# First input chunks in three transfers on two queues, zero-padded kv and wo, two products left over in the last block, in a gated attention and MLP kernel

## The chip, the core and the metric

The kernel runs on one core of a Trainium2 chip. What counts is the device time of one execution in microseconds (us). Before the change it is 435.35 us, the median of three runs (435.15 to 435.68).

The engines are named as in the profile: PE multiplies matrices and writes PSUM, PEld is its loading of weights, DVE, ACT and POOL work element by element, SP issues most transfers from memory. A row with a q behind the engine (SPq, ACTq) is an instruction of that engine's sequencer, here a transfer being issued.

## The reference

2048 rows of 448 floats go through a linear attention (16 heads of 28) and through an MLP with 1792 hidden columns and a squared ReLU; a sigmoid gate mixes both.

```python
g = sigmoid((x * gate_w).sum(-1, keepdims=True))
q, k, v = split(x @ wqkv)                       # 16 heads of 28
phi = lambda t: where(t > 0, t + 1, exp(t)) + 1e-6
kv  = einsum("bhsd,bhse->bhde", phi(k), v)
z   = phi(k).sum over s
o   = (phi(q) @ kv) / (phi(q) . z + 1e-6)
a   = o.reshape(B, S, D) @ wo
h   = relu(x @ w1 + b1)
b   = (h * h) @ w2 + b2
return g * a + (1 - g) * b
```

## The kernel before, in words

Everything is float32, and each operand of a product is split into two float32r halves, a high part (a conversion, `split_hi`, L63) and a low part (the subtraction of it, `split_lo`, L71). A product is then three terms: high by high, high by low, low by high. The 448 input columns are four chunks of 128 rows (`c` = 0 to 3); the fourth holds its 64 columns twice, with both parts stacked, and needs two terms. So one tile of hidden columns is 11 matmuls of 512 columns (`up`, L241, through `up_chunk`, L218), and the same 11 terms occur in queries, keys and attention.

The rows go in four blocks of 512 (`b`, `TB` = 512, `NB` = 4). In a first pass each block makes the first seven of 14 tiles of hidden columns: `up`, then `hidden` (L231: ReLU and square on ACT, split on DVE), then `down` (L260: 12 matmuls of 448 columns into four PSUM banks `o_ps`). Between them stand the keys (`keys`, L291) and the sums of phi(k) times x (`gram`, L331). After the pass `kv_product` (L397) makes kv; `split_kv` splits it, and `m_product` (L431) multiplies it by a quarter of wo four times, three matmuls each, into the matrix `m_s` that `attention` (L512) uses. In the second pass, in the order 3, 0, 1, 2, each block makes the other seven tiles, its queries (`queries`, L447), denominators and attention, and `finish` (L275) writes the rows out. `n` counts the blocks of the second pass and `fl` the tiles in one.

The order on PE, ACT and DVE is that of the code. SP and POOL are placed by the scheduler of the tile framework, which also hands out eight semaphores for transfers in turn: the ninth issue waits until the first has landed. `down` queues its 12 matmuls in a list (`owed`), and `leave` says how many of them stay in the list until the next `down`; they then run behind the next `up`. The tables `leaves` (L616 for the first pass, L683 for the second) give that number by block and tile.

The start, on which much of the change bears: PE first runs 14 matmuls on constants (L177). Two transfers `xw` (L184 to L187), 256 KB each, bring half the columns of x's chunk 0 beside half the columns of the first weights' chunk 0. ACT converts the x half, DVE the weight half, and four matmuls of 256 columns (L547) follow, for two tiles by two column halves. The other products of chunk 0 are ordered by terms (for `n`, L555), those of chunks 1 to 3 tile by tile (L559). `split_x` (L111) and `split_w1` (L141) convert chunks 1 to 3, high parts on ACT and low parts on DVE.

kv has 112 rows a head group (`JE`), so the tiles `kv_h`, `kv_l`, `woh` and `wol` have 112 partitions.

Of the kernel before, what the change touches and what calls it, by code (L numbers as in the profile page):

```python
# [7 lines left out]
F = mybir.dt.float32  # L8
# [7 lines left out]
P = 128  # L16
TB = 512
# [10 lines left out]


@with_exitstack  # L30
def gated_mix_kernel(ctx: ExitStack, tc: tile.TileContext, xw, xt, xn, wk, wq, wv, wo, w1a, w1b, w2, b1, b2, gw,
                     hmask, kvmask, halves, out):
    nc = tc.nc
    act, dve, pool, pe, sp = nc.scalar, nc.vector, nc.gpsimd, nc.tensor, nc.sync
# [93 lines left out]

    w1_s, w1_raw = {}, {}

    def load_w1(h, g, c):
        w1_raw[h, g, c] = slot([P, (TB, 3 * P)[g]], F, f"w1r{h}{g}{c}")
        load(w1_raw[h, g, c], (w1a, w1b)[g][h, c])

    def new_w1(h, g):
        n, a, z = ((TB, 0, 16), (3 * P, 48, 0))[g]
# [39 lines left out]
    for _ in range(14):  # L176
        pe.matmul(warm_ps[:, :256], warm[:, :P], warm, start=True, stop=True)  # L177

    side = rest.tile([P, 56], F, name="side")[:, :2]
    dve.memset(side[:64, 0:1], -1.0)  # L180
    dve.memset(side[:64, 1:2], 0.0)
    dve.memset(side[64:], 1.0)

    xw_raw = []  # L184
    for n in range(2):
        xw_raw.append(slot([P, TB], F, f"xwr{n}"))
        load(xw_raw[n], xw[n])  # L187
    for c in range(1, 4):
        load_x(0, c)
        load_w1(0, 0, c)  # L190
    b1_s = keep.tile([P, NF], F, name="b1_s")
    half = keep.tile([P, 2], F, name="half")
    ones = keep.tile([P, 2], F, name="ones")
# [193 lines left out]
    def load_kv(c):  # L387
        if c == 0:
            kvm.append(slot([JE, D], F, "kvm"))
            load(kvm[0], kvmask)  # L390
        wv_s.append(slot([P, D], F, f"wv{c}"))
        load(wv_s[-1], wv[c])

    def kv_product():
        kv_ps = bank("kv_ps")
        z_ps = mm_p.tile([P, 512], F, name="z_ps", tag="mm")
        for c in range(4):  # L397
            pe.matmul(z_ps[:, 2 * c:2 * c + 2], zks[0][:, c].rearrange("p j r -> p (j r)"), ones, start=True,  # L398
                      stop=True)
        dve.tensor_copy(zc, z_ps[:, 0:8:2])  # L400
        for j in range(NJ):
            js = slice(j * JE, (j + 1) * JE)
            for c in range(4):
                pe.matmul(kv_ps[:JE, js], wv_s[c][:, js], gsum[c][:, js], start=(c == 0), stop=(c == 3))  # L404
        raw = slot([JE, D], F, "kv_raw")
        dve.tensor_tensor(raw, kv_ps[:JE, :D], kvm[0], op=ALU.mult)
        return raw.rearrange("p (j k) -> p j k", j=NJ)

    def split_kv(raw):
        kv.extend([late_tile([JE, NJ, P], "kv_h"), late_tile([JE, NJ, P], "kv_l")])  # L410
        split_hi(act, kv[0][:, :, :JE], raw)
        split_lo(dve, kv[1][:, :, :JE], raw, kv[0][:, :, :JE])
        for t in kv:
            dve.tensor_copy(t[:, :, JE:], f32(t[:, :, 96:JE]))

    def late_tile(shape, name, dt=R):
        return late.tile(shape, dt, name=name, tag="q", bufs=NLATE)
# [1 line left out]
    wo_raw, wo_s = {}, {}  # L419

    def load_wo(j):
        wo_raw[j] = slot([JE, D], F, f"wor{j}")
        load(wo_raw[j], wo[j])

    def split_wo(j):
        wo_s[j] = [late_tile([JE, TB], f"wo{p}{j}")[:, 16:16 + D] for p in "hl"]
        raw = wo_raw.pop(j)
        split_hi(act, wo_s[j][0], raw)
        split_lo(dve, wo_s[j][1], raw, wo_s[j][0])
# [104 lines left out]

    first = [mm_p.tile([P, 512], F, name=f"h_ps0_{f}", tag="mm") if f < 2 else bank(f"h_ps0_{f}") for f in range(4)]
    for c in range(4):
        if c == 0:
            xs[0] = new_x(0)  # L540
            w, (xh, xl) = new_w1(0, 0), [x[:, 0] for x in xs[0]]
            sides = slice(0, TB // 2), slice(TB // 2, TB)
            for n, cols in enumerate(sides):
                split_hi(act, xh[:, cols], xw_raw[n][:, sides[0]])
                split_hi(dve, w[:, 0, cols], xw_raw[n][:, sides[1]])
                for f in range(2):
                    pe.matmul(first[f][:, cols], w[:, 0, f * P:(f + 1) * P], xh[:, cols], start=(n == 0), stop=False)  # L547
            for m, (lo, hi) in enumerate(((xl, xh), (w[:, 4], w[:, 0]))):
                for n, cols in enumerate(sides):
                    split_lo(dve, lo[:, cols], xw_raw[n][:, sides[m]], hi[:, cols])  # L550
        else:
            split_x(0, c)
            split_w1(0, 0, c)
        if c == 0:
            for n in range(3):  # L555
                for f in range(0 if n else 2, 4):
                    up_chunk(first[f], 0, f, c, n)
        else:
            for f in range(4):  # L559
                up_chunk(first[f], 0, f, c)  # L560
    split_w2(0)
    split_w2(1)
    wk_s = keep.tile([P, 7, D], R, name="wk_s", tag="wkm", bufs=1)
# [116 lines left out]


    order = [NB - 1, *range(NB - 1)]
    leaves = (0, 1, 2, 0, 1, 2, 0), (0, 1, 2, 0, 0, 0, 2)  # L683
    late = m_s = None
    for n, b in enumerate(order):
        then = order[n + 1] if n + 1 < NB else None
        for f in range(NF - NH, NF):
            fl = f - NH
            run_todo()
            if fl == (0 if n else 4) and n != 1:  # L690
                split_den(b)
            up(b, f)
            if then is not None and n and fl < 2:
                load_x(then, 2 * fl)
                load_x(then, 2 * fl + 1)
            if n == 0:
                if 1 <= fl < 3:
                    load_x(then, 2 * fl - 2)
                    load_x(then, 2 * fl - 1)
                if fl == 1:  # L700
                    for c in range(4):
                        split_w1(1, 1, c)
                    for j in range(2, 4):
                        load_wo(j)
                if 1 <= fl < 5:
                    split_wo(fl - 1)
                if fl < 2:
                    load_w2(NH + 5 + fl)
                if fl < 3:
                    split_w2(NH + 4 + fl)  # L710
                if 2 <= fl < 4:
                    split_x(then, 2 * fl - 4)
                    split_x(then, 2 * fl - 3)
            elif then is not None and 1 <= fl < 3:
                split_x(then, 2 * fl - 2)
                split_x(then, 2 * fl - 1)
            if fl:
                if n + 1 < NB or f + 1 < NF:
                    down(b, f - 1, leave=leaves[min(n, 1)][fl])
            elif n == 0:  # L720
                down(b, NH - 1)
                half_done(b)
            else:
                down(order[n - 1], NF - 1)
                for i in range(4):
                    if n == 1:
                        attention(order[0], i)
                        if i == 1:
                            split_den(b)
                    finish(order[n - 1], i)  # L730
            if n == 0:
                if fl < 4:
                    todo += queries(b, (3, 0, 1, 2)[fl])
                if fl == 0:
                    for c in range(4):
                        load_w1(1, 1, c)
                    raw = kv_product()
                    phase1.close()
                    late = ctx.enter_context(tc.tile_pool(name="late", bufs=1, side="right", reuse_waits="tile"))
                    m_s = keep.tile([P, 7, D], R, name="m_s", tag="wkm", bufs=1)  # L740
                    split_kv(raw)
                    for j in range(2):
                        load_wo(j)
                if fl == 4:
                    m_product(2)
                if fl in (2, 3, 5):
                    m_product(fl - 2)
                for c in ((0,), (1, 2, 3))[fl - 5] if fl >= 5 else ():
                    scaled(b, c)
                if fl >= 4:  # L750
                    for c in ((3,), (0,), (1, 2))[fl - 4]:
                        todo += queries(then, c)
                if fl == 4:
                    todo += denominators(b)
            else:
                if fl == 0:
                    todo += denominators(b)
                if 2 <= fl < 4:
                    scaled(b, 2 * fl - 4)
# [69 lines left out]
```

## Time and profile before

| | us |
|---|---|
| median of three runs | 435.35 (435.15 to 435.68) |
| the profiled execution | 435.59 |
| its span, first to last instruction | 433.8 |
| PE busy in the span | 429.5 (99%) |
| DVE, ACT, POOL busy | 283.7, 174.5, 72.1 |

The profiled execution is 0.24 us above the median, and 1.8 us of it lie outside the span. Busy time of PE is the union of matmuls that overlap: a matmul of 512 columns is shown with some 390 ns, but the next one starts 227 ns after it. So a stretch of PE is best read by the starts of its matmuls, or by the chain of work that ended last, which gives the time that each run of matmuls added.

### The profile page before, as it was taken

How to read it: one execution, taken by the hardware profiler on the slowest of the kernel's cores; microseconds unless marked ns; L12 is line 12 of the kernel's file. 1: busy time of each engine (PE TensorE's matmuls, PEld its weight loads, DVE VectorE, ACT ScalarE, POOL GpSimd, SP SyncE). 2: the span in 40 equal slices, each digit the busy share in tenths (PEclk: the TensorE clock that was granted, in tenths of full speed). 3: DMA queues.
4: the chain of work that ended last, by engine and by line, in shares of the span. 5: the costliest groups of instructions: out<-in, count | busy, mean ns of one | idle time of the engine just before them, and what ended most of it. 6: DMA issues, size and time to landing. Idle time of an engine off the chain costs nothing.

```text
span 433.8 us, 5561 instructions
## 1 busy us (share of the span) xinstructions
PE 429.5 (99%) x2052; PEld 381.4 (88%) x2052; DVE 283.7 (65%) x462; ACT 174.5 (40%) x302; POOL 72.1 (17%) x93
## 2 busy tenths in 40 slices
PE   9999999999999999999999999999999999999996
PEld 7898999898989899898898888988888888888986
DVE  5899518843499437784449777887653967457624
ACT  6865324421346122453145443444433434233421
POOL 0045006500065002540010441000100001000000
PEclk9999999999999999999999999999999999999999
DMA  7741302020221211223244321130101301002002
GB/s 282 240 134 51 109 0 69 27 68 1 70 82 65 72 45 48 65 58 111 63 118 134 69 65 38 61 122 0 26 0 48 136 0 26 0 0 86 0 2 85
DMA packets 18347, 29.00 MB, mean 67 GB/s; under 512 B 2896, under 2 KB 12672, under 8 KB 18320
## 3 DMA queue, kind: packets, MB, share of 16 engines
q1 hardware_dynamic: 16416, 26.35, 19.5%
q0 software_dynamic: 1760, 2.20, 2.3%
q8 instruction: 16, 0.26, 0.3%
q14 instruction: 11, 0.09, 0.1%
q10 hardware_dynamic: 144, 0.10, 0.1%
HBM read 22.31 MB, written 3.67 MB: 60 GB/s over the span
## 4 chain that ended last, share of the span: by engine, by line
PE 98%; DMA 1%; DVE 0%; ACT 0%; DVEq 0%; issue 0%
PE h_ps L229 32%; PE o_ps L254 31%; PE q_ps L84 8%; PE k_ps L254 8%; PE a_ps L84 8%; PE g_ps L84 8%; PE kv_ps L404 1%; DMA xwr<-in_xw 1%; PE m_ps L84 1%; PE d_ps L84 0%; PE h_ps L547 0%; PE z_ps L398 0%; DVE out L278 0%; ACT xh L65 0%; DVEq L825 0%
## 5 line engine op out<-in xcount | busy, mean ns | idle before, releaser
L254 PE MATMUL o_ps<-w,hh 128*128 128x448 f32 x448 | 128.6, 362 | 0.0
L229 PE MATMUL h_ps<-xh,w 128*128 128x512 f32 x390 | 124.8, 391 | 0.0
L254 PEld LDWEIGHTS o_ps<-w,hh 128*128 128x128 f32 x448 | 84.0, 187 | 7.7
L229 PE MATMUL h_ps<-xl,w 128*128 128x512 f32 x224 | 87.0, 391 | 0.0
L229 PEld LDWEIGHTS h_ps<-xh,w 128*128 128x128 f32 x390 | 73.4, 188 | 14.1
L254 PE MATMUL o_ps<-w,hl 128*128 128x448 f32 x224 | 81.2, 362 | 0.0
L233 ACT ACTIVATE hr<-h_ps,b_s 128x512 f32<-128x512 f32 x56 | 38.1, 680 | 86.1 <-PE h_ps L229 80.8
L69 DVE CAST hh<-hr 128x512 fp32r<-128x512 f32 x56 | 23.5, 420 | 61.8 <-ACT hr L234 61.7
L229 PEld LDWEIGHTS h_ps<-xl,w 128*128 128x128 f32 x224 | 42.4, 189 | 8.0
L254 PEld LDWEIGHTS o_ps<-w,hl 128*128 128x128 f32 x224 | 42.0, 188 | 3.7
L72 DVE TENSOR_TENSOR hl<-hr,hh 128x512 fp32r<-128x512 f32 x56 | 39.7, 709 | 3.3
L72 POOL TENSOR_TENSOR nl<-xnr,nh 128x384 fp32r<-128x384 f32 x16 | 17.2, 1076 | 119.0 <-ACT nh L65 118.9
L234 ACT ACTIVATE hr<-hr 128x512 f32<-128x512 f32 x56 | 35.4, 632 | 1.8
L84 PE MATMUL q_ps<-xh,wq_s 128*128 128x512 f32 x100 | 33.1, 390 | 0.0
L84 PE MATMUL a_ps<-m_s,qh 128*128 128x448 f32 x112 | 32.7, 362 | 0.0
L254 PE MATMUL k_ps<-wk_s,xh 128*128 128x448 f32 x112 | 32.7, 361 | 0.0
L474 POOL DMA_DIRECT2D qr<-qv x16 | 7.9, 503 | 124.3 <-ACT qv L471 94.5
L72 DVE TENSOR_TENSOR pl<-r,ph 128x448 fp32r<-128x448 f32 x16 | 23.7, 1479 | 0.0
L327 POOL TENSOR_TENSOR ksum<-ksum,r 128x448 f32<-128x448 f32 x15 | 23.3, 1555 | 1.1 <-DVE r L289 1.1
L84 PE MATMUL q_ps<-xl,wq_s 128*128 128x512 f32 x60 | 23.4, 389 | 0.0
L254 PE MATMUL k_ps<-wk_s,xl 128*128 128x448 f32 x64 | 23.2, 363 | 0.0
L84 PE MATMUL a_ps<-m_s,ql 128*128 128x448 f32 x64 | 23.2, 362 | 0.0
(111 smaller groups left out, 565.8 us busy)
## 6 DMA issues: line engine op xcount, KB each, us to landing
xr<-in_xt SPq DMA_DIRECT2D x27, 256.0 KB, 2.7
xnr<-in_xn SPq DMA_DIRECT2D x16, 224.0 KB, 2.5
out<-out SPq DMA_DIRECT2D x15, 224.0 KB, 1.9
w2r<-in_w SPq DMA_DIRECT2D x14, 224.0 KB, 2.7
w1r<-in_w1a SPq DMA_DIRECT2D x7, 256.0 KB, 2.7
w1r<-in_w1b SPq DMA_DIRECT2D x8, 192.0 KB, 3.3
m_s<-m POOLq DMA_DIRECT2D x12, 112.0 KB, 2.5
wqr<-in_wq SPq DMA_DIRECT2D x4, 256.0 KB, 2.7
```

Source lines behind the costliest of these rows:

```text
L69: eng.tensor_copy(hi, src)
L72: eng.tensor_tensor(lo, src, f32(hi), op=ALU.subtract)
L84: pe.matmul(out_ps, a, b, start=(i == 0), stop=(i == n - 1))
L229: pe.matmul(ps, a, m, start=(c == 0 and n == 0), stop=(c == 3 and n == 1))
L233: act.activation(r, ps, AF.Relu, bias=b1_s[:, f:f + 1])
L234: act.activation(r, r, AF.Square)
L254: pe.matmul(ps, a, m, start=start, stop=stop)
L327: pool.tensor_tensor(ksum, ksum, p, op=ALU.add)
L404: pe.matmul(kv_ps[:JE, js], wv_s[c][:, js], gsum[c][:, js], start=(c == 0), stop=(c == 3))
L474: pool.dma_start(out=r[p + 16:p + 32], in_=v[p:p + 16])
```

## The change

There are six edits.

- **Three transfers at the start.** `xw0` and `xw1` have 192 KB: half the columns of x's chunk 0 and 128 columns of the first weights. The other 256 weight columns come as a third transfer, `w1c`, 128 KB, issued by ACT, and ACT also issues the next weight chunk (`w1r` of chunk 1). Ahead of both ACT runs a small activation into two spare columns, which brings the load of its function table to the front.
- **Conversions at the start.** x's chunk 0 is now converted by DVE and the weights' by ACT, in three pieces. The first four matmuls go tile by tile instead of half by half.
- **Chunk 1 by terms.** Chunk 1's x is converted by DVE, its weights by ACT in two pieces, and its 12 matmuls are ordered by terms, as those of chunk 0 were.
- **128 rows for kv and wo.** The tiles get 16 rows of zeros, from a memset for kv and from padded memory for wo. The mask of kv is loaded by POOL instead of SP.
- **Two m products earlier.** `m_product(0)` and `m_product(1)` stand ahead of the queries of their tile instead of behind.
- **Two products left over.** In the last block the fifth and sixth tiles leave two matmuls of `down` for later, as the table `leaves` has them.

```diff
     xw_raw = []
-    for n in range(2):
-        xw_raw.append(slot([P, TB], F, f"xwr{n}"))
-        load(xw_raw[n], xw[n])
+    for n, src in enumerate((xw0, xw1, w1c)):
+        xw_raw.append(slot([P, src.shape[1]], F, f"xwr{n}"))
+        if n < 2:
+            load(xw_raw[n], src)
+        else:
+            act.activation(spare, nc.const_aps.tensor(1.0, (P, 2), F), AF.Copy)
+            act.dma_start(out=xw_raw[n], in_=src)
+            load_w1(0, 0, 1, act)
     for c in range(1, 4):
         load_x(0, c)
-        load_w1(0, 0, c)
+        if c > 1:
+            load_w1(0, 0, c)
...
-            load(kvm[0], kvmask)
+            pool.dma_start(out=kvm[0], in_=kvmask)
...
-        raw = slot([JE, D], F, "kv_raw")
-        dve.tensor_tensor(raw, kv_ps[:JE, :D], kvm[0], op=ALU.mult)
+        raw = slot([P, D], F, "kv_raw")
+        dve.memset(raw[96:], 0.0)
+        dve.tensor_tensor(raw[:JE], kv_ps[:JE, :D], kvm[0], op=ALU.mult)
...
-            sides = slice(0, TB // 2), slice(TB // 2, TB)
-            for n, cols in enumerate(sides):
-                split_hi(act, xh[:, cols], xw_raw[n][:, sides[0]])
-                split_hi(dve, w[:, 0, cols], xw_raw[n][:, sides[1]])
-                for f in range(2):
-                    pe.matmul(first[f][:, cols], w[:, 0, f * P:(f + 1) * P], xh[:, cols], start=(n == 0), stop=False)
...
+            hx = TB // 2
+            xcols, wcols = (slice(0, hx), slice(hx, TB)), (slice(0, P), slice(P, 2 * P), slice(2 * P, TB))
+            for n in range(2):
+                split_hi(dve, xh[:, xcols[n]], xw_raw[n][:, :hx])
+                split_hi(act, w[:, 0, wcols[n]], xw_raw[n][:, hx:])
+            split_hi(act, w[:, 0, wcols[2]], xw_raw[2])
+            for f, n in ((0, 0), (0, 1), (1, 0), (1, 1)):
+                pe.matmul(first[f][:, xcols[n]], w[:, 0, wcols[f]], xh[:, xcols[n]], start=(n == 0), stop=False)
...
+        elif c == 1:
+            (xh, xl), w, rx, rw = xs[0], w1_s[0, 0], x_raw[0, 1], w1_raw.pop((0, 0, 1))
+            split_hi(dve, xh[:, 1], rx)
+            for cols in (slice(0, 2 * P), slice(2 * P, TB)):
+                split_hi(act, w[:, 1, cols], rw[:, cols])
+            split_lo(dve, xl[:, 1], rx, xh[:, 1])
+            split_lo(dve, w[:, 5], rw, w[:, 1])
...
+        for n in range(3) if c < 2 else (None,):
+            for f in range(2 if (c, n) == (0, 0) else 0, 4):
+                up_chunk(first[f], 0, f, c, n)
...
-    leaves = (0, 1, 2, 0, 1, 2, 0), (0, 1, 2, 0, 0, 0, 2)
+    leaves = (0, 1, 2, 0, 1, 2, 0), (0, 1, 2, 0, 0, 0, 2), (0, 1, 2, 0, 0, 0, 2), (0, 1, 2, 0, 2, 2)
...
-                    down(b, f - 1, leave=leaves[min(n, 1)][fl])
+                    down(b, f - 1, leave=leaves[n][fl])
...
             if n == 0:
+                if fl in (2, 3):
+                    m_product(fl - 2)
                 if fl < 4:
                     todo += queries(b, (3, 0, 1, 2)[fl])
```

What the scheduler makes of the transfers does not stand in the diff. SP's first issues before are these (`xwr` the first two transfers, `xr` and `w1r` the chunks of x and of the first weights, `b_s` the bias b1):

```order
L58 DMA xwr_110<-in_xw 128x512
L58 DMA xwr_112<-in_xw 128x512
L58 DMA xr_1_114<-in_xt 128x512
L58 DMA w1r_116<-in_w1a 128x512
L58 DMA xr_2_118<-in_xt 128x512
L58 DMA w1r_120<-in_w1a 128x512
L58 DMA xr_3_122<-in_xt 128x512
L58 DMA w1r_124<-in_w1a 128x512
L58 DMA b_s<-in_b 128x14
```

SP's first issues now (`gw_s` the gate's weights, 224 KB, which before came far later, behind the key weights):

```order
L58 DMA xwr_110<-in_xw 128x384
L58 DMA xwr_112<-in_xw 128x384
L58 DMA b_s<-in_b 128x14
L58 DMA gw_s<-in_gw 128x448
L58 DMA xr_1_119<-in_xt 128x512
L58 DMA xr_2_121<-in_xt 128x512
L133 DMA w1r_123<-in_w1a 128x512
L58 DMA xr_3_125<-in_xt 128x512
L133 DMA w1r_127<-in_w1a 128x512
```

The bias and the gate's weights now stand between the first two transfers and x's chunk 1. ACT's first instructions now, the first of them the load of its function table:

```order
L191 ACT_TABLE_LOAD
L191 ACTIVATE side<-const-float32-1.0 128x2
L192 DMA xwr_114<-in_w1c 128x256
L133 DMA w1r_117<-in_w1a 128x512
L65 ACTIVATE w_00_174<-xwr_110 128x128
L65 ACTIVATE w_00_174<-xwr_112 128x128
L65 ACTIVATE w_00_174<-xwr_114 128x256
L65 ACTIVATE w_00_174<-w1r_117 128x256 x2
```

Before, ACT began with the same table load and then converted x (`xh`), and issued nothing. On PE, around the first m product in the second pass, the rows now are (`o_ps` a product of `down`, `q_ps` of the queries):

```order
L261 MATMUL o_ps3_7_3_2122<-w2_8_1831,hh3_8_2089 128x448
L84 MATMUL m_ps0_2205<-woh0_2110,kv_h_2055 128x448
L84 MATMUL m_ps0_2205<-wol0_2111,kv_h_2055 128x448
L84 MATMUL m_ps0_2205<-woh0_2110,kv_l_2056 128x448
L84 MATMUL q_ps3_1_2217<-xh3_1327,wq_s_167 128x512
L84 MATMUL q_ps3_1_2217<-xl3_1328,wq_s_167 128x512
```

Before, the three `m_ps` rows stood behind the queries' eleven matmuls, between them and the next `h_ps`.

## Rows read from the trace of the kernel before

**Rows 1.** The page: busy time of the engines, granted clock, chain by engine.

```profile
PE 429.5 (99%) x2052; PEld 381.4 (88%) x2052; DVE 283.7 (65%) x462; ACT 174.5 (40%) x302; POOL 72.1 (17%) x93
...
PEclk9999999999999999999999999999999999999999
...
PE 98%; DMA 1%; DVE 0%; ACT 0%; DVEq 0%; issue 0%
```

**Rows 2.** Chain that ended last, in time, the start: start us, us, what.

```profile
3.98 1.39 PE h_ps L547 x4
5.37 10.20 PE h_ps L229 x42
15.57 2.21 PE k_ps L254 x11
```

**Rows 3.** Timeline of PE, 3.4 to 8.5 us: start us, us, instruction, count.

```profile
3.08 0.84 PE L177 MATMUL warm_ps<-const-bfloat16-1.0 128*128 128x256 bf16 x3
...
5.17 1.05 PE L229 MATMUL h_ps<-xh,w 128*128 128x512 f32 x2
6.02 1.38 PE L229 MATMUL h_ps<-xl,w 128*128 128x512 f32 x4
7.24 1.31 PE L229 MATMUL h_ps<-xh,w 128*128 128x512 f32 x5
8.38 0.39 PE L229 MATMUL h_ps<-xl,w 128*128 128x512 f32 x1
```

**Rows 4.** Timeline of ACT, DVE and SP, 0 to 16 us; in brackets idle before, releaser.

```profile
0.74 1.28 ACT L65 ACT_TABLE_LOAD   x1 [0.74 <-PEq L821]
0.74 0.85 SPq L58 DMA_DIRECT2D xwr<-in_xw  x2
...
3.51 0.42 ACT L65 ACTIVATE xh<-xwr 128x256 fp32r<-128x256 f32 x1 [1.49 <-DMA xwr<-in_xw]
3.51 0.29 DVE L69 CAST w<-xwr 128x256 fp32r<-128x256 f32 x1 [2.40 <-DMA xwr<-in_xw]
...
4.11 0.42 ACT L65 ACTIVATE xh<-xwr 128x256 fp32r<-128x256 f32 x1 [0.18 <-DMA xwr<-in_xw]
...
5.96 0.63 ACT L65 ACTIVATE xh<-xr 128x512 fp32r<-128x512 f32 x1 [1.44 <-DMA xr<-in_xt]
...
12.77 2.34 DVE L72 TENSOR_TENSOR wk_s<-wkr,wk_s 128x448 fp32r<-128x448 f32 x4
```

**Rows 5.** Timeline of POOL, 136 to 152 us.

```profile
137.99 1.59 POOL L327 TENSOR_TENSOR ksum<-ksum,r 128x448 f32<-128x448 f32 x1
139.51 0.70 POOL L662 DMA_DIRECT2D hmr<-in_hmask  x1
```

**Rows 6.** Chain in time, around the four m products.

```profile
233.21 2.49 PE q_ps L84 x11
235.70 0.61 PE m_ps L84 x3
236.31 2.51 PE h_ps L229 x11
...
250.06 1.63 PE q_ps L84 x7
...
257.47 2.55 PE q_ps L84 x11
```

**Rows 7.** Chain in time, the last block.

```profile
413.70 2.54 PE h_ps L229 x11
```

**Rows 8.** Groups by line and shape: count, busy us, mean ns, idle before.

```profile
L84 PEld LDWEIGHTS m_ps<-woh,kv_h 112*128 112x128 f32 x4 | 0.8, 188 | 0.1
```

**Rows 9.** The mask's tile: its load (duration ns, first and last start us), DVE's idle before its use.

```profile
L58 SPq DMA_DIRECT2D kvm<-in_kvmask x1: 342/342/342, 193.5 to 193.5; - x1
L406 DVE TENSOR_TENSOR kv_raw<-kv_ps,kvm x1: 625/625/625, 221.3 to 221.3; 112x448 f32<-112x448 f32 x1
...
  PE kv_ps L404: 3.1, 1
```

More of the change, by code (lines that the diff above doesn't have):

```diff
@@ L30, in gated_mix_kernel @@
 @with_exitstack
-def gated_mix_kernel(ctx: ExitStack, tc: tile.TileContext, xw, xt, xn, wk, wq, wv, wo, w1a, w1b, w2, b1, b2, gw,
+def gated_mix_kernel(ctx: ExitStack, tc: tile.TileContext, xw0, xw1, w1c, xt, xn, wk, wq, wv, wo, w1a, w1b, w2, b1, b2, gw,
                      hmask, kvmask, halves, out):
@@ L129, in gated_mix_kernel, with load_w1 @@
     w1_s, w1_raw = {}, {}
-    def load_w1(h, g, c):
+    def load_w1(h, g, c, queue=sp):
         w1_raw[h, g, c] = slot([P, (TB, 3 * P)[g]], F, f"w1r{h}{g}{c}")
-        load(w1_raw[h, g, c], (w1a, w1b)[g][h, c])
+        queue.dma_start(out=w1_raw[h, g, c], in_=(w1a, w1b)[g][h, c])
     def new_w1(h, g):
@@ L177, in gated_mix_kernel @@
         pe.matmul(warm_ps[:, :256], warm[:, :P], warm, start=True, stop=True)
-    side = rest.tile([P, 56], F, name="side")[:, :2]
+    side, spare = [t[:, n:n + 2] for t in [rest.tile([P, 56], F, name="side")] for n in (0, 2)]
     dve.memset(side[:64, 0:1], -1.0)
@@ L404, in kv_product @@
                 pe.matmul(kv_ps[:JE, js], wv_s[c][:, js], gsum[c][:, js], start=(c == 0), stop=(c == 3))
-        raw = slot([JE, D], F, "kv_raw")
-        dve.tensor_tensor(raw, kv_ps[:JE, :D], kvm[0], op=ALU.mult)
+        raw = slot([P, D], F, "kv_raw")
+        dve.memset(raw[96:], 0.0)
+        dve.tensor_tensor(raw[:JE], kv_ps[:JE, :D], kvm[0], op=ALU.mult)
         return raw.rearrange("p (j k) -> p j k", j=NJ)
     def split_kv(raw):
-        kv.extend([late_tile([JE, NJ, P], "kv_h"), late_tile([JE, NJ, P], "kv_l")])
+        kv.extend([late_tile([P, NJ, P], "kv_h"), late_tile([P, NJ, P], "kv_l")])
         split_hi(act, kv[0][:, :, :JE], raw)
@@ L421, in load_wo @@
     def load_wo(j):
-        wo_raw[j] = slot([JE, D], F, f"wor{j}")
+        wo_raw[j] = slot([P, D], F, f"wor{j}")
         load(wo_raw[j], wo[j])
     def split_wo(j):
-        wo_s[j] = [late_tile([JE, TB], f"wo{p}{j}")[:, 16:16 + D] for p in "hl"]
+        wo_s[j] = [late_tile([P, TB], f"wo{p}{j}")[:, 16:16 + D] for p in "hl"]
         raw = wo_raw.pop(j)
@@ L541, in gated_mix_kernel @@
             w, (xh, xl) = new_w1(0, 0), [x[:, 0] for x in xs[0]]
-            sides = slice(0, TB // 2), slice(TB // 2, TB)
-            for n, cols in enumerate(sides):
-                split_hi(act, xh[:, cols], xw_raw[n][:, sides[0]])
-                split_hi(dve, w[:, 0, cols], xw_raw[n][:, sides[1]])
-                for f in range(2):
-                    pe.matmul(first[f][:, cols], w[:, 0, f * P:(f + 1) * P], xh[:, cols], start=(n == 0), stop=False)
-            for m, (lo, hi) in enumerate(((xl, xh), (w[:, 4], w[:, 0]))):
-                for n, cols in enumerate(sides):
-                    split_lo(dve, lo[:, cols], xw_raw[n][:, sides[m]], hi[:, cols])
+            hx = TB // 2
[6 more added lines that the diff above has]
+                pe.matmul(first[f][:, xcols[n]], w[:, 0, wcols[f]], xh[:, xcols[n]], start=(n == 0), stop=False)
+            for n in range(2):
+                split_lo(dve, xl[:, xcols[n]], xw_raw[n][:, :hx], xh[:, xcols[n]])
+            for n, raw in enumerate((xw_raw[0][:, hx:], xw_raw[1][:, hx:], xw_raw[2])):
+                split_lo(dve, w[:, 4, wcols[n]], raw, w[:, 0, wcols[n]])
+        elif c == 1:
[5 more added lines that the diff above has]
+            split_lo(dve, w[:, 5], rw, w[:, 1])
         else:
@@ L553, in gated_mix_kernel @@
             split_w1(0, 0, c)
[L554 to L560, printed above, removed]
+        for n in range(3) if c < 2 else (None,):
+            for f in range(2 if (c, n) == (0, 0) else 0, 4):
+                up_chunk(first[f], 0, f, c, n)
     split_w2(0)
@@ L745, in gated_mix_kernel @@
                     m_product(2)
-                if fl in (2, 3, 5):
-                    m_product(fl - 2)
+                if fl == 5:
+                    m_product(3)
                 for c in ((0,), (1, 2, 3))[fl - 5] if fl >= 5 else ():
@@ L801 @@
     a = {
-        "xw": np.stack([np.concatenate([t[:, n * TB // 2:(n + 1) * TB // 2] for t in (xt[0, 0], w1[0, 0])], axis=1)
-                        for n in range(2)]),
+        "xw0": np.concatenate([xt[0, 0, :, :TB // 2], w1[0, 0, :, :P]], axis=1),
+        "xw1": np.concatenate([xt[0, 0, :, TB // 2:], w1[0, 0, :, P:2 * P]], axis=1),
+        "w1c": w1[0, 0, :, 2 * P:TB],
         "xt": xt,
@@ L808 @@
         "wv": v_w[twice].reshape(4, P, D),
-        "wo": inputs["A_wo"].reshape(NJ, JE, D),
+        "wo": np.pad(inputs["A_wo"].reshape(NJ, JE, D), ((0, 0), (0, P - JE), (0, 0))),
         "w1a": w1[..., :TB],
```

## The prediction

> **What bounds the kernel now.** I read the page first, then the chain of work that ended last in order of time, then the timeline of the first microseconds. The page says PE: 99% busy, 98% of the chain [rows 1]. Busy time alone would not prove it, since matmuls overlap in the record, so I went through the chain in time. From 3.98 us on it is matmuls without a break: 42 of 512 columns take 10.20 us, 11 of 448 take 2.21 [rows 2], and all through the middle a run of 11 takes 2.49 (512 columns) or 2.2 us (448) [rows 2, 6], run behind run. In the middle PE waits for no other engine by more than hundredths of a microsecond. Two ends are left, and small seams.
>
> The start: the first data lands at 3.51 [rows 4] and the first real product starts at 3.98 [rows 2]. From there PE is at half pace: two products of 512 columns take the time from 5.17 to 6.02, 0.427 us each, which is 1.2 GHz. The four of "xl" fill 6.02 to 7.24, 0.305 each, so the pace changes among them, near 6.6; the five from 7.24 to 8.38 take 0.228 each, which is 2.4 GHz [rows 3]. The granted clock reads full in every fortieth of the span [rows 1], so it does not show the early stretch; the pace is read from the starts. What the change gains ahead of about 6.6 us is therefore worth only 227/427, about half.
>
> The most that can be had is soon summed. An unbroken half-pace stretch from the last warm-up product on (its last three begin at 3.08 [rows 3], at 0.213 each for 256 columns: 3.08 + 0.64 = 3.72) would save 0.26 us of waiting, and the four first products take 1.19 us (3.98 to 5.17) where four of 256 columns at 0.213 need 0.85, another 0.34; together 0.60, at half pace 0.32 us. The seams below hold 0.23. So without a change of the clock the bound on the gain is some 0.55 us, 0.13%, under the 0.2% (0.87 us) that a measurement of this kernel can tell from no change. The question is how much can be lost.
>
> **Part 1, the start.** Pace of landing: the second 256 KB land 0.60 us after the first (3.51, 4.11) [rows 4]. With 192 KB the first lands about 0.15 earlier, 3.36, the second 0.30 earlier, 3.81. DVE converts 256 columns in 0.29; ACT's 256 columns take 0.42 and 512 take 0.63 [rows 4], so 128 take about 0.31. First product at 3.36 + 0.31 + 0.04 = 3.71, behind the warm-up at 3.72. The next three need the second transfer: 3.81 + 0.31 + 0.04 = 4.16, 4.37, 4.59; end 4.80, where before it was 5.17. Then comes tile 2, and it needs the third transfer, which has no row: none is issued by ACT early in the trace.
>
> Lower bound: it is there in time, tile 2 at 4.80, a gain of 0.37 at half pace, 0.20 us. Between: ACT's issue waits behind the table load (0.74 + 1.28 = 2.02) and an activation of some 0.2 us. The nearest row of an issue behind running work is POOL's: the mask's issue starts at 139.51, where the addition ahead of it ends at 139.58 [rows 5]. Then the third issue is at 2.2; the first transfer took 2.77 from issue to landing (0.74 to 3.51) [rows 4] and this one has half the bytes, 0.30 less, so it lands at 4.67 to 4.97; with 0.42 for 256 columns and 0.04, tile 2 starts at 5.13 to 5.43: from 0.02 us gained to 0.14 lost. I take **0.05 lost**. The upper end is rival 1.
>
> A page of the Trainium skill, "DMA: Bandwidth & Descriptors", section "Issuing engines are not separate DMA queues", speaks against the gain: transfers of SP, ACT and POOL run on the same 16 engines and interleave, and a second issuer saves only issue time. By that rule the term is rival 1's; no row of before has two queues busy at the start.
>
> **Part 2, chunk 1.** Its x moves behind the bias and the gate's weights on SP: two more issues of 0.43 ahead, less one (its weights are on ACT now), and 231 KB, about 0.54 at the pace above. It landed at 5.96 [rows 4]; say 6.5 to 6.9 now. DVE's conversion of 512 columns (about 0.43) ends by 7.4. Chunk 1's first product stood at 8.38 - 0.23 = 8.15 [rows 3]. Cover 0.8 us: **no cost**. If x's chunk 1 lands after 7.7, each further microsecond costs its full length, since PE is at full pace then. The order by terms makes the low parts due 4 and 8 products later (0.9 and 1.8 us) instead of 1 and 2, so DVE's extra conversions are covered. What follows on SP, the key weights among it, moves by the same half microsecond. DVE ends their low parts at 15.11 (12.77 + 2.34) [rows 4], so at 15.6; the last of the four is needed by the tenth of the eleven key products, which begin near 15.4, so after 17. Covered.
>
> **Part 3, 128 rows.** Three m products take 0.61 us instead of 0.60, four times, and the run behind them is long: 2.51 against 2.49 twice, 1.63 for seven against 1.585, 2.55 against 2.49 [rows 6]. Sum 0.04 + 0.02 + 0.02 + 0.045 + 0.06 = about 0.18 us. If the 112 rows are the cause all of it goes; if not, none. The same excess of 0.05 stands in the last block at 413.70 with no 112-row operand near [rows 7], which speaks for another cause of at least a part. I take half: **0.09 gained**. Sixteen more rows add no columns, and the conversions go by columns (0.42 and 0.63 above). The memset of kv's zeros lies in DVE's 3.1 us of idle time ahead of the mask product, and the mask, issued by SP at 193.5 [rows 9], is now issued by POOL behind the key sums, some 28 us before that product (221.3) [rows 9]. Each is nothing; without that cover the memset would cost DVE some 0.3 us and PE still nothing, since the split of kv is first used 12 us later.
>
> On the load of weights, "TensorE: Matmul & The Clock Gate", section "LDWEIGHTS (loading the stationary operand)", says that its time goes by columns, not by rows. The row agrees: the load of 112 rows takes 188 ns [rows 8], as the others do. By that rule the term would be 0, and the sum 0.09 higher.
>
> **Part 4, order.** The m products of the first two tiles come 2.49 us earlier. Their operands: wo's and kv's parts are split a tile earlier. ACT and DVE keep their order, so the queries' results reach ACT 0.6 us later and m's earlier; PE waits for neither at once. Nothing. The leftovers in the last block: 24 matmuls change places, none is added; at best the 0.05 at 413.70 goes, at worst nothing changes. **0.02 gained**.
>
> **Sum.** 435.59 + 0.05 - 0.09 - 0.02 = 435.53 for the profiled execution, which is 0.24 above the median: **435.3 us**.
>
> **Rivals.** (1) The new queue takes its share from the first two transfers. If ACT's sequencer issues at once, at about 0.9 and 1.3, its 384 KB are in the engines beside SP's 384. The second transfer then lands with 768 KB moved instead of 512: at 0.60 per 256 KB that is 4.71, and by the next landing of before, x's chunk 1 (third in the queue), as late as 5.96 [rows 4]. Then products 2 to 4 start at 5.06 to 6.31, tile 2 three products (0.64) later at 5.70 to 6.95 instead of 5.17: 0.53 to 1.78 at half pace, 0.28 to 0.95 us. Time 435.5 to 436.2. For it: the table load runs on the engine, and nothing shows that it holds up the sequencer. Against: the POOL row. Chance 25%.
>
> (2) Slower: the clock rises later. Up to its rise in before PE was never without products for more than 0.26 us (3.72 to 3.98). With rival 1's late second transfer it idles from 3.9 to 5.1 or more. If the rise then slips, each microsecond of it costs 1 - 227/427 = 0.47 us. It decides from a slip of 1.2 us on, when with rival 1's 0.35 it passes 436.22; at 3 us it gives 437.0. Chance 10%.
>
> (3) Faster: with no gap at 3.72 the clock rises earlier. 2 us would give 0.94, 434.4. Against: the warm-up products are as before and begin at the same time. Chance 8%.
>
> **How the numbers follow.** Forecast 57%, rivals 25, 10 and 8. Forecast and rival 1 lie within 0.2% but for 2 of rival 1's 25. So faster 0.08, same 0.80, slower 0.12. The range reaches down to 434.5, which leaves out most of rival 3, and up to 436.4, which takes in all of rival 1 and leaves out most of rival 2.
>
> **What would show it.** In the trace after: first real product at 3.7; the next three at 4.2 (forecast) or past 5 (rival 1); ACT's issues at 2.2 or at 0.9; chunk 1's first product without a gap ahead of it; products at 227 ns from some 6.6 us on, or later (rival 2). The runs of 11 behind the m products at 2.49 if the rows were the cause. Wrong would be the whole view if in the middle of the kernel PE waits somewhere where it did not, most likely at x's chunk 1 or in the last block.

## The result: slower by 0.37%, and the profile after

The changed kernel takes 437.06 us (median of 22 runs, 436.57 to 438.69) against 435.47 us of the kernel before beside it (22 runs, 434.76 to 437.66). The ratio is 1.0037, with a 95% interval of 1.003 to 1.0044: slower by some 1.6 us, outside the predicted range of 434.5 to 436.4. The profiled execution took 437.14 us, with a span of 435.4 us.

On the page of the changed kernel, first the engines' busy time, then the chain's shares by engine, then a group of matmuls with its count, busy us, mean ns and the idle time ahead of it:

```profile
PE 430.3 (99%) x2052; PEld 381.8 (88%) x2052; DVE 284.3 (65%) x465; ACT 174.3 (40%) x304; POOL 72.6 (17%) x94
...
PE 97%; DMA 2%; SPq 0%; DVE 0%; issue 0%; DVEq 0%
...
L236 PE MATMUL h_ps<-xh,w 128*128 128x512 f32 x390 | 124.8, 391 | 0.4 <-DVE xh L69 0.4
```

PE bounds the kernel as in [rows 1], but the chain now spends 2% on transfers, and one group of matmuls waits for DVE's conversion of x. The chain in order of time (start us, us, what) says where. First its start, then its last pieces:

```profile
2.59 6.64 DMA xr<-in_xt
...
9.83 7.54 PE h_ps L236 x32
17.37 2.21 PE k_ps L261 x11
...
426.71 5.21 PE o_ps L261 x26
431.93 0.02 issue
```

Before, the chain ran through PE from 3.98 us on [rows 2]. Now it goes back to the transfer of x's chunk 1 (`xr`), which is issued at 2.59 and lands at 9.23. The keys (`k_ps`) start at 17.37 instead of 15.57 [rows 2]: 1.80 us lost in the first 18 us. From there to the end of the last matmul it takes 431.93 - 17.37 = 414.56 us. Before, that was 414.79: the chain of before has these last pieces.

```profile
425.54 4.82 PE o_ps L254 x24
430.36 0.03 issue
```

430.36 - 15.57 = 414.79. So the middle gained 0.23 and the start lost 1.80, which leaves 1.57; the profiled executions differ by 1.55.

The timeline of the changed kernel's first microseconds (start us, us, instruction, count, and in brackets idle before and releaser), first ACT and SP, then DVE and PE:

```profile
0.74 1.28 ACT L191 ACT_TABLE_LOAD   x1 [0.74 <-PEq L840]
...
0.80 0.38 ACTq L192 DMA_DIRECT2D xwr<-in_w1c  x1
...
2.12 0.43 SPq L58 DMA_DIRECT2D gw_s<-in_gw  x1
...
3.40 0.29 DVE L69 CAST xh<-xwr 128x256 fp32r<-128x256 f32 x1 [2.28 <-DMA xwr<-in_xw]
...
3.84 0.55 PE L559 MATMUL h_ps<-xh,w 128*128 128x256 f32 x1
...
4.43 0.29 DVE L69 CAST xh<-xwr 128x256 fp32r<-128x256 f32 x1 [0.74 <-DMA xwr<-in_xw]
...
4.79 1.01 PE L559 MATMUL h_ps<-xh,w 128*128 128x256 f32 x3 [0.39 <-DVE xh L69]
...
5.59 1.05 PE L236 MATMUL h_ps<-xh,w 128*128 128x512 f32 x2
...
6.44 1.91 PE L236 MATMUL h_ps<-xl,w 128*128 128x512 f32 x4
...
8.15 1.27 PE L236 MATMUL h_ps<-xh,w 128*128 128x512 f32 x4
...
9.26 0.43 DVE L69 CAST xh<-xr 128x512 fp32r<-128x512 f32 x1 [3.12 <-DMA xr<-in_xt]
...
9.83 1.17 PE L236 MATMUL h_ps<-xh,w 128*128 128x512 f32 x4 [0.41 <-DVE xh L69]
```

Three things are to be seen. ACT issues its transfer at 0.80, while the table load runs. Products of 512 columns go at half pace (the 1.2 GHz level) until past 8.15, 0.427 us each from 6.44 on ((8.15 - 6.44) / 4), where before the pace changed near 6.6 [rows 3]. And chunk 1's first product starts at 9.83, behind a wait for x, where before it stood at 8.15. That is 1.68 of the 1.80 us; the other 0.12 are in the 32 products behind the wait, 7.54 us where before they took 7.42 (15.57 - 8.15).

### The profile page after: what moved, and what is told of

Its sections match the earlier page's. It is cut to its first block, busy times and chain, and to the rows that moved or that the text cites. A ratio compares the mean times of both kernels' runs of the same rounds, so it can differ in the third digit from the quotient of the medians.

```text
span 435.4 us, 5568 instructions
## 1 busy us (share of the span) xinstructions
PE 430.3 (99%) x2052; PEld 381.8 (88%) x2052; DVE 284.3 (65%) x465; ACT 174.3 (40%) x304; POOL 72.6 (17%) x94
## 4 chain that ended last, share of the span: by engine, by line
PE 97%; DMA 2%; SPq 0%; DVE 0%; issue 0%; DVEq 0%
PE h_ps L236 32%; PE o_ps L261 31%; PE q_ps L84 8%; PE a_ps L84 8%; PE g_ps L84 8%; PE k_ps L261 8%; DMA xr<-in_xt 2%; PE kv_ps L412 1%; PE m_ps L84 1%; PE d_ps L84 0%; SPq L58 0%; PE z_ps L406 0%; DVE out L285 0%; DVE xh L69 0%; DVEq L844 0%
```

## The experiments

The question is which of the two sets the loss, the late landing of x's chunk 1 or the late rise of the clock, and what makes the chunk late: a second queue, more bytes ahead of it, or the gate's weights (`gw_s`), a load that reads one row of memory 128 times.

**The repeated loads held back.** The changed kernel; the loads of the gate's weights and of b2 wait for a memset behind chunk 1's conversions.

```diff
             split_lo(dve, w[:, 5], rw, w[:, 1])
+            for t in (gw_s, b2_s):
+                dve.memset(t[:, :2], 0.0)
```

> The changed kernel, but the two loads that read one row of memory 128 times (the gate's weights and b2) are held back until chunk 1 is converted; SP then issues the bias and a 1 KB table in their place. Theory A (the repeated-row load of the gate's weights, ahead of x's chunk 1 on SP, slows the transfers): x's chunk 1 lands at 6.0 to 7.2 us instead of 9.24, no wait of PE ahead of chunk 1, 0.6 to 1.5 us faster than the changed kernel: 435.6 to 436.5. Theory B (the second queue splits the 16 engines, so x's chunk 1 comes late whatever stands ahead of it): it lands past 8.5 and the time stays within 0.4 of the changed kernel's 437.1.

Measured: 435.64 us (10 runs, 434.65 to 436.88), ratio to before 1.0002 [0.9986, 1.0018]. The loss is gone from the median. Six runs lie between 434.65 and 435.83, four between 436.81 and 436.88. The kernel before, beside it, also has runs that long, four of 31 from 436.76 up. The profiled execution is one of the four of the held kernel (436.81). Its timeline, DVE and PE:

```profile
6.29 0.43 DVE L69 CAST xh<-xr 128x512 fp32r<-128x512 f32 x1
...
4.03 0.55 PE L559 MATMUL h_ps<-xh,w 128*128 128x256 f32 x1
5.00 1.01 PE L559 MATMUL h_ps<-xh,w 128*128 128x256 f32 x3 [0.41 <-DVE xh L69]
...
6.66 1.91 PE L236 MATMUL h_ps<-xl,w 128*128 128x512 f32 x4
8.37 2.33 PE L236 MATMUL h_ps<-xh,w 128*128 128x512 f32 x8
```

x's chunk 1 is there by 6.29 (DVE converts it without a wait), as theory A expected, and PE does not wait at chunk 1. What is late in this execution is the clock: half pace until past 8.37. PE stood idle from 4.24 (4.03 + 0.21) to 5.00 before that.

**The same bytes from 128 rows.** The changed kernel; memory holds the gate's weights 128 times, so that the load, at the same place and of the same 224 KB, reads 128 rows.

```diff
-    load(gw_s, gw.partition_broadcast(P))
+    load(gw_s, gw)
```

> The changed kernel with the gate's weights stored 128 times in memory, so that the same 224 KB at the same place in SP's queue come from 128 different rows. Theory A1 (the repeated row is slow, its bytes are not): transfers run near 380 KB per us through 4 to 7 us, x's chunk 1 lands at 6.5 to 7.5, 0.6 to 1.5 us faster than the changed kernel: 435.6 to 436.5. Theory A2 (224 KB ahead of it are the cost, wherever they come from) or theory B (the second queue): x's chunk 1 lands past 8.5, time within 0.4 of 437.1.

Measured: 435.35 us (10 runs, 434.72 to 437.65; seven of them at most 435.55, three from 436.83 up), ratio 1.0006 [0.9989, 1.0022]. Its chain at the start (profiled at 435.55):

```profile
2.59 5.09 DMA xr<-in_xt
...
8.27 7.52 PE h_ps L236 x32
```

The chunk lands at 7.67 instead of 9.23, a little past the 6.5 to 7.5 of theory A1 and well short of A2's 8.5. Between these two executions the repetition alone makes 1.56 us; the landing itself varies from execution to execution (8.83 with the repeated row in a kernel below). The rates show how. The table by stretches gives each engine's busy share, the granted clock, the share of busy DMA engines and GB/s; here is the stretch from 5 to 6 us, first of the changed kernel, then of this one.

```profile
5.00:6.00 1.00, 1.00 (x4) 0.92 (x5) 1.00 (x5) 0.67 (x3) 0.00 (x0) 1.00 0.90 91
```
```profile
5.00:6.00 1.00, 1.00 (x7) 0.86 (x7) 1.00 (x5) 0.67 (x3) 0.00 (x0) 1.00 1.01 385
```

The DMA engines are about as busy in these two executions, 0.90 against 1.01, and move 91 GB/s instead of 385. PE in this execution:

```profile
4.79 0.62 PE L559 MATMUL h_ps<-xh,w 128*128 128x256 f32 x3 [0.26 <-DVE xh L69]
5.25 0.63 PE L236 MATMUL h_ps<-xh,w 128*128 128x512 f32 x2
```

The first product began at 4.01, so at half pace PE stood idle from 4.22 to 4.79, and yet the two products of 512 columns from 5.25 on take 0.23 us each, which is full pace: here an idle stretch did not make the clock late.

**All on one queue.** The changed kernel; `w1c` and the weights of chunk 1 are issued by SP. The scheduler then leaves the gate's weights far back.

```diff
-            act.dma_start(out=xw_raw[n], in_=src)
-            load_w1(0, 0, 1, act)
+            sp.dma_start(out=xw_raw[n], in_=src)
+            load_w1(0, 0, 1, sp)
```

> The changed kernel with the third transfer and chunk 1's weights issued by SP, behind the first two; the scheduler then leaves the gate's weights far back. Theories A and B alike: x's chunk 1 no later than 6.5 us, faster than the changed kernel by 1.4 us or more: 435.7 or less. Against held-back loads on two queues it tells the queue's part: by theory A alone the same within 0.3; if the second queue delays the second of the first transfers (4.43 now, 4.11 before), here it lands by 3.9, tile 2 starts near 4.8 to 5.0, and the time is 0.2 to 0.9 lower than with two queues.

Measured: 435.26 us (10 runs, 434.94 to 437.33; four of them from 437.04 up), ratio 1.0 [0.9981, 1.0019]. ACT's timeline (profiled at 437.29, one of those four):

```profile
3.18 0.31 ACT L65 ACTIVATE w<-xwr 128x128 fp32r<-128x128 f32 x1 [0.94 <-DMA xwr<-in_xw]
3.74 0.31 ACT L65 ACTIVATE w<-xwr 128x128 fp32r<-128x128 f32 x1 [0.25 <-DMA xwr<-in_xw]
5.61 0.42 ACT L65 ACTIVATE w<-xwr 128x256 fp32r<-128x256 f32 x1 [1.56 <-DMA xwr<-in_w1c]
```

And DVE's conversion of x's chunk 1:

```profile
7.26 0.43 DVE L69 CAST xh<-xr 128x512 fp32r<-128x512 f32 x1 [0.78 <-DMA xr<-in_xt]
```

Alone on their queue the first two transfers land at 3.18 and 3.74, where beside ACT's queue they landed at 3.40 and 4.43. But the third comes at 5.59, so PE again stands idle, here ahead of tile 2, which starts at 6.08 instead of the expected 4.8 to 5.0. x's chunk 1 lands at 7.26, later than the expected 6.5, with no repeated row ahead of it; PE, still at half pace up to 8.81 (the products from 7.10 on take 0.43 us each), does not wait for it. The order of arrival moves; the start as a whole gains nothing that can be measured.

**The start of before, all middle edits.** The changed kernel's 128 rows, m order, leftovers and mask, with the start as before.

```diff
-    for n, src in enumerate((xw0, xw1, w1c)):
+    for n in range(2):
+        xw_raw.append(slot([P, TB], F, f"xwr{n}"))
+        load(xw_raw[n], xw[n])
...
```

> The kernel before with the changes of the middle alone (128 rows for kv and wo, mask on POOL, two m products earlier, two products left over); its start is that of before. The trace of the changed kernel gains 0.23 us between the key sums' product and the end, so 0.2 us faster than before if that stands by itself; the seams behind the m products and in the last block at 2.49 us. No gain would say that the 0.23 came from the start.

Measured: 435.40 us (10 runs, 434.72 to 436.0), ratio 0.9996 [0.9986, 1.0006]. The difference of 0.2 us is below what can be told from no change by the times, but the chain shows it: keys at 15.24, last matmul's end at 429.79, 414.55 us where before took 414.79.

**Before with the gate's weights early.** The kernel before with one move: b1 and the gate's weights ahead of x's chunk 1, all on SP.

```diff
+    b1_s = keep.tile([P, NF], F, name="b1_s")
+    load(b1_s, b1)
+    gw_s = keep.tile([P, D], F, name="gw_s")
+    load(gw_s, gw.partition_broadcast(P))
     for c in range(1, 4):
         load_x(0, c)
         load_w1(0, 0, c)
```

> The kernel before with one edit: the bias b1 and the gate's weights (one memory row read 128 times, 224 KB) are loaded ahead of x's chunk 1; all is on SP's one queue, and the start is otherwise that of before. Theory A (the load of the repeated row is slow and holds up what is queued behind it): x's chunk 1 lands near 8.5 to 9.5 us instead of 5.96, PE waits ahead of the first product of chunk 1, and the time is 0.8 to 1.8 us above before. Theory B (the second queue on ACT is what slows x's chunk 1): it lands near 6.6, half a microsecond later for 231 KB more, PE does not wait, and the time is within 0.3 us of before.

Measured: 437.53 us (4 runs, 437.12 to 439.08), ratio 1.0052 [1.0036, 1.0069]. Its chain, and the stretch from 4 to 5 us in the table by stretches:

```profile
2.59 6.08 DMA xr<-in_xt
...
9.98 7.83 PE h_ps L230 x32
17.81 2.21 PE k_ps L255 x11
```
```profile
4.00:5.00 1.00, 1.00 (x4) 0.91 (x5) 0.96 (x4) 0.42 (x1) 0.00 (x0) 1.00 0.26 76
```

No second queue is busy, full pace begins before 6 us (four products from 5.75 to 6.66, 0.23 us each), and the loss is there: 1.95 us by the medians, a little larger than that of the change and than the 1.8 at most that was expected. x's chunk 1 lands at 8.67, sooner than in the changed kernel, but ACT then converts x and the weights one after the other (0.63 and 0.62 us), so that the first product starts at 9.98, after 2.25 us of waiting. So the place of this one load (b1's 7 KB moved with it) is enough to make the loss. The second queue is not needed for it.

**128 rows alone, leftovers alone.** Two kernels, each the kernel before with one middle edit.

```diff
-        raw = slot([JE, D], F, "kv_raw")
+        raw = slot([P, D], F, "kv_raw")
+        dve.memset(raw[96:], 0.0)
...
-        wo_raw[j] = slot([JE, D], F, f"wor{j}")
+        wo_raw[j] = slot([P, D], F, f"wor{j}")
```

> The kernel before with 128 rows (16 of zeros) for kv and wo, and nothing else. The middle of the kernel, from the key and value product to the last matmul, took 208.92 us before and 208.69 with all middle edits. If the 112 rows are the cause of the long runs behind the m products: the four runs after them take 2.49 (1.59 for seven) instead of 2.51, 1.63, 2.51 and 2.55, and the middle takes 208.73 to 208.76. If the place of the m products ahead of the queries is the cause: the runs stay as they were and the middle takes 208.87 or more.

```diff
-    leaves = (0, 1, 2, 0, 1, 2, 0), (0, 1, 2, 0, 0, 0, 2)
+    leaves = (0, 1, 2, 0, 1, 2, 0), (0, 1, 2, 0, 0, 0, 2), (0, 1, 2, 0, 0, 0, 2), (0, 1, 2, 0, 2, 2)
```

> The kernel before with the table of leftovers of the change (two products left over twice in the last block), and nothing else. If the leftovers take away the seam of the last block: the run that took 2.54 there takes 2.49, and the middle of the kernel takes 208.87 instead of 208.92 us. If not: 208.92, and 2.54 somewhere in the last block. No measurable change of the time in either case.

Measured with one execution each, 435.51 and 434.94 us, within the spread of the kernel before (434.76 to 437.66 in 22 runs); their chains decide. With 128 rows alone, around the m products and at the end:

```profile
236.33 2.52 PE h_ps L229 x11
...
250.08 1.59 PE q_ps L84 x7
...
257.43 2.49 PE q_ps L84 x11
...
425.44 4.82 PE o_ps L254 x24
```

Against [rows 6] the two runs of queries behind m products are short now (1.59 for 1.63, 2.49 for 2.55), the two of `h_ps` stay long (2.52 both, of which one is shown, for 2.51). From the keys (15.59) to the end of the last matmul (425.44 + 4.82) it takes 414.67, 0.12 less than before: between the 0.16 to 0.19 expected if the rows were the whole cause and the 0.05 at most if the place was. With the leftovers alone, in the last block:

```profile
412.70 2.49 PE h_ps L229 x11
...
424.50 5.21 PE o_ps L254 x26
```

The run that took 2.54 [rows 7] takes 2.49, and keys (14.98) to end (429.71) take 414.73 to 414.74, 0.05 less. All edits give 0.23 to 0.24, so some 0.06 is left for the order of the m products (and the mask's load on POOL), by difference: neither was run alone, but in the chain of all middle edits the runs of `h_ps` take 2.49.

**PE kept busy between the first products.** Three kernels with more products on constants. First the held kernel above with six: two at the end of the warm-up, four between the first product and the second.

```diff
-    for _ in range(14):
+    for _ in range(16):
...
                 pe.matmul(first[f][:, xcols[n]], w[:, 0, wcols[f]], xh[:, xcols[n]], start=(n == 0), stop=False)
+                if (f, n) == (0, 0):
+                    for _ in range(4):
+                        pe.matmul(warm_ps[:, :256], warm[:, :P], warm, start=True, stop=True)
```

> The changed kernel with the loads of the gate's weights and b2 held back (as in the run after_held, whose times fell into two groups, near 434.8 and near 436.8, and whose profiled execution of the second group ran at half pace up to 9.05 us), and six more products on constants on PE: two at the end of the warm-up and four between the first product and the second, where PE stood idle for 0.8 us. Theory clock (an idle PE between the first product and the next is what lets the clock rise late): all runs fall near 434.6 to 435.0, none near 436.8, and the pace is 0.23 us for 512 columns from 7 us on at the latest. Theory data (the two groups come from when the transfers land): the two groups stay as they were. If a late rise happens for a reason that PE's own work does not set, the upper group stays too, with transfers landing as in after_held.

Measured: 435.20 us (11 runs, 434.61 to 435.90), ratio 0.9991 [0.9982, 1.0]. The group at 436.8 is gone: none of 11, where it was 4 of 10, though the runs reach 435.90, not only the expected 435.0. PE's timeline (profiled at 434.98):

```profile
4.37 0.75 PE L562 MATMUL warm_ps<-const-bfloat16-1.0 128*128 128x256 bf16 x4
5.05 0.62 PE L559 MATMUL h_ps<-xh,w 128*128 128x256 f32 x3
...
5.97 1.09 PE L236 MATMUL h_ps<-xl,w 128*128 128x512 f32 x4
6.89 1.99 PE L236 MATMUL h_ps<-xh,w 128*128 128x512 f32 x8
```

0.23 us for each product of 512 columns from 5.97 on: full pace, although chunk 0's data came no earlier than in the held kernel (DVE's second conversion at 4.70 against 4.65). So a late clock does not follow from the data's time, and with PE kept busy it was not seen. That the idle time of PE is its cause is likely but not shown: the two kernels ran on different chips, and on this one the kernel before had no such run either (none of 15 above 435.97, where beside the held kernel it had four of 31). And in the kernel that loads the gate's weights from 128 rows PE stood idle too, with the clock early.

Then the same six products in the changed kernel itself, loads as they are.

> The changed kernel, loads as they are, with the six added products on constants of held_filled (two at the end of the warm-up, four between the first product and the second). Theory A (the landing of x's chunk 1 sets the loss, and the late clock is hidden behind it): full pace comes early, PE waits longer ahead of chunk 1's first product, which still starts near 9.8 us, and the time stays within 0.3 us of the changed kernel's 437.06. Rival (the late rise of the clock sets the loss): the time falls to 435.0 to 435.5, as held_filled's did.

Measured: 436.79 us (10 runs, 436.33 to 438.58), ratio 1.0029 [1.0016, 1.0042]. PE and chain (profiled at 436.69):

```profile
5.76 1.09 PE L236 MATMUL h_ps<-xl,w 128*128 128x512 f32 x4
6.69 1.08 PE L236 MATMUL h_ps<-xh,w 128*128 128x512 f32 x4
9.42 1.17 PE L236 MATMUL h_ps<-xh,w 128*128 128x512 f32 x4 [1.65 <-DVE xh L69]
```
```profile
2.60 6.23 DMA xr<-in_xt
...
16.94 2.21 PE k_ps L261 x11
```

Full pace comes 3 us sooner than in the changed kernel, or more, and the time falls by only 0.27 us: PE waits 1.65 us for the chunk instead of 0.41. Even that gain need not be the clock's, since the chunk landed 0.40 sooner in this execution, at 8.83 (its first product at 9.42 instead of the expected 9.8). This tells the two causes apart. The landing of x's chunk 1 sets the loss, and the late clock lies hidden behind it.

Last, the start of before with all middle edits and two such products, one at the end of the warm-up, one between the two halves of the first four.

```diff
-    for _ in range(14):
+    for _ in range(15):
...
                     pe.matmul(first[f][:, cols], w[:, 0, f * P:(f + 1) * P], xh[:, cols], start=(n == 0), stop=False)
+                if n == 0:
+                    pe.matmul(warm_ps[:, :256], warm[:, :P], warm, start=True, stop=True)
```

> The start of before with all middle edits (as mid_only, 435.40), and two more products on constants: one at the end of the warm-up, which ends at 3.72 us where the first product starts at 3.98, and one between the two halves of the first four products. Theory clock (idle time of PE before the first products lets the clock rise late): full pace by 6 us in all runs, times of 434.6 to 435.2, median near 434.9, 0.1 to 0.2% below before. Rival (what is left of idle time there does not matter): median 435.2 to 435.5, as mid_only, or 0.1 us more for the two products at half pace.

Measured: 435.20 us (12 runs, 434.81 to 435.72), ratio 0.9986 [0.9978, 0.9995] to the kernel before beside it (435.64). It is the one kernel here whose whole interval lies below 1, by 0.14%. The median of 434.9 that was expected did not come (435.20 is the edge of the rival's 435.2 to 435.5), and the interval overlaps that of the same kernel without the two products, so what they add is not settled. In its trace full pace came before 6 us (0.23 us for each product of 512 columns from 5.31 on), and the chain then went through the weights of chunk 1, which landed at 6.81: the data set the start there, not the clock.

## Why the prediction was wrong, by its own steps

**The step that failed is part 2's "no cost".** It put x's chunk 1 at 6.5 to 6.9 by pricing the gate's weights at their bytes: 231 KB, 0.54 us at the pace of the first two transfers. The chunk landed at 9.23. The place was right (it named a landing past 7.7 as the point from which each microsecond costs its full length, and x's chunk 1 as the likeliest place of a wait), and by that rule 9.23 costs 1.53, against 1.68 measured. What was missing is that this load, which reads one row 128 times, takes far longer than its bytes at that pace. The trace of before had this price. Its transfers table gives the median us from issue to landing in the last column, and its table by stretches has here first a microsecond not long after the gate's weights and b2 were issued (11.12 and 11.68), then one shortly before they landed (near 17.0 and 17.8):

```profile
gw_s<-in_gw SPq DMA_DIRECT2D x1, 224.0 KB, 5.9
```
```profile
13.00:14.00 1.00, 1.00 (x6) 0.84 (x5) 1.00 (x3) 0.38 (x1) 0.00 (x0) 1.00 1.08 399
...
15.00:16.00 1.00, 1.00 (x6) 0.89 (x5) 0.47 (x2) 1.00 (x2) 0.00 (x0) 1.00 1.03 102
```

399 GB/s fall to 102 with the DMA engines as busy as before. At 15 us PE was not waiting, so no view of waits showed it; ahead of the chunk that PE needs next it costs its whole length. An estimate from these rows: 231 KB at 100 GB/s are 2.3 us instead of 0.54, so a landing of 8.2 to 8.7 and a loss of 0.5 to 1.0 us. Still short, but on the right side.

A smaller step of part 2 was misread as well: it counted two issues more ahead of the chunk, "less one" for the weights that moved to ACT. Those weights stood behind the chunk on SP, not ahead of it, so its issue slipped by both, from 1.64 to 2.59 us. What the slip of 0.95 costs by itself is not shown; in the held kernel, with the same issue time, the chunk was there by 6.29.

**The rest of 9.23 is only partly settled.** With 128 rows instead of one the chunk landed at 7.67, and with almost nothing there (1 KB) at 6.29 or sooner. So 223 KB of plain rows still cost 1.38 us or more, where the pace of the first transfers gives 0.52. A hint lies in the tables by stretches: 258 GB/s up to 7.67 in the first of these kernels and 237 GB/s up to 6.29 in the other are 1.98 and 1.49 MB, a difference of 0.49 MB, about twice the 223 KB. The other half is most likely loads issued behind the chunk that were moved before it had landed; at 385 GB/s it makes some 0.7 us, as an estimate, most of what is missing. No run here shows why they came between.

**Part 1, the start: rival 1 had the mechanism, and the times lie between it and the forecast.** The POOL row, from which I took that an issue waits behind running work, does not carry over to ACT: its issue went out at 0.80, beside the table load. The second transfer landed at 4.43 (forecast 3.81, rival 1 from 4.71), products 2 to 4 began at 4.79 (4.16 to 4.59; from 5.06), tile 2 at 5.59 (5.13 to 5.43; from 5.70). All three are nearer rival 1, whose times were some 0.1 to 0.3 us too late. On one queue the second landed at 3.74. The page of the Trainium skill that the prediction named, "DMA: Bandwidth & Descriptors", section "Issuing engines are not separate DMA queues", has transfers of all issuers interleave on the same engines, and these landings agree. Only the first product's time was near, 3.84 for 3.71. None of it counted in the end, since PE waited for x's chunk 1 anyway.

**Rival 2, the later clock, happened in the profiled execution but was not the loss.** Half pace lasted some 2 us longer than in the trace of before. That is more than the 1.2 us from which the rival was to decide, but behind it stood the longer wait for the chunk, as the kernel with six more products shows. Where the chunk was early, in the held kernel, the one late run that was profiled had the late clock, and four of ten times were some 2 us above the best of the others; the rival's 0.47 us for each microsecond gives 1.2 for its slip to past 9 us against 6.6. Of its mechanism the idle stretch is shown and, as said, its part as the cause is not. That the measured 437.06 is close to the 437.0 which rival 2 names for a slip of 3 us is luck: the slip was 2 us, and the time came from the chunk.

**Part 3 was mis-sized.** 0.09 was taken between 0 and 0.18. The 128 rows alone gained 0.12, the order of the m products some 0.06 by difference, where it was put at nothing. The excess of 0.05 in the last block, from which the doubt was drawn, was a seam of its own. The weight load takes 187 to 188 ns with 128 rows, as with 112 [rows 8]. That agrees with the Trainium skill, page "TensorE: Matmul & The Clock Gate", section "LDWEIGHTS (loading the stationary operand)", by which its time does not go by rows. But the term was not 0: the loss showed in the runs of products behind (1.63 to 1.59, 2.55 to 2.49).

**Part 4.** The leftovers gained 0.05, the upper bound; 0.02 was taken. The later key weights cost PE nothing, as foreseen: the middle of the changed kernel took 414.56 us, that of all middle edits on the old start 414.55. Nor did the memset and the mask on POOL: in the changed kernel the memset took 0.43 us of DVE, which then still waited 2.5 us for PE ahead of the mask product at 223.1, and the mask, issued at 195.8, landed 3.5 us later.

In sum: middle 0.23 gained for 0.11 forecast, start 1.80 lost for 0.05.

## What to carry to other kernels

When an edit lets a scheduler pull a load forward, price that load by its own row, from issue to landing and by the GB/s of the stretch in which it ran, not by its bytes, and ask what stands behind it in its queue. A load that reads one row for all partitions can be harmless late and cost its full length early; keep it behind the transfers that PE is waiting for. Two causes in the same stretch are told apart by taking away one at a time: the products on constants took away the late clock and left nearly all of the loss.

## What the runs showed that was not expected

- A load that reads one memory row 128 times: the gate's 224 KB took 4.6 to 6.5 us from issue to landing over the traces here (6.5 in the changed kernel, 4.1 there with 128 rows). While it ran the core's DMA engines moved 91 GB/s in the changed kernel (385 with 128 rows). Their busy share is no sign of it: 0.90 there, 0.48 at 103 GB/s in the kernel with six more products, 0.26 at 76 GB/s in the kernel before with the load early.
- ACT's sequencer issues transfers (0.80 and 1.22) while its engine loads a function table (0.74 to 2.02).
- Where PE stood idle for 0.6 to 1.2 us among the first products and x's chunk 1 was not very late, the executions of one kernel fell in two groups (434.65 to 435.83 and 436.81 to 437.65 over three kernels of ten runs, eleven of the 30 in the upper one; four of 31 for the kernel before on that chip); with products on constants in that gap eleven runs, on another chip, fell in one, 434.61 to 435.90.
- A third transfer behind two others on one queue, 128 KB, took 3.94 us from issue (1.65) to landing (5.59), with no repeated row ahead of it. Why is open.
